# Packed attention with a mixture of experts on one core: the maxima's joining, the exponentials and the gates' chain moved among the work items

## The chip, the cores and the metric

The kernel runs on one core of a Trainium2 chip. The metric is the device time of one execution in microseconds (us). TensorE (PE), VectorE (DVE), ScalarE (ACT), GpSimd (POOL) and SyncE (SP, which issues most of the loads and stores) each work through their own list of instructions in order and wait for each other by semaphores. PEld in the views is TensorE's loading of weights, which runs beside its matmuls.

## The reference

```python
def sm_attn(qq, kk, vv):
    s = scale * np.matmul(qq, kk.transpose(0, 1, 3, 2))
    s = s - np.max(s, axis=-1, keepdims=True)
    a = np.exp(s)
    a = a / (np.sum(a, axis=-1, keepdims=True) + 1e-09)
    return np.matmul(a, vv)
p_packed = sm_attn(p, k, v)          # p: 32 rows a head; k, v: 576 rows
out = sm_attn(q, p_packed, p_packed) # 8 batches, 8 heads, 576 rows, 64 columns
...
logits = xn @ en.T / tau             # x: out as 4608 rows of 512
expert_idx = np.argmax(logits, axis=1)
...
h = np.maximum(x[mask] @ w1[e], 0.0)            # 512 -> 1024
out[mask] = gate_w[mask, None] * (h @ w2[e])    # 1024 -> 512
```

Everything is float32. xn and en are the normalised rows and expert embeddings; gate_w is the largest of the softmax over the 8 experts.

## The kernel before, in words

The eight batches are worked one after the other, and two of them overlap: while the FFN of batch b runs (the generator `ffn`), the attention of batch b+1 (`att_main`) is issued in small pieces between its pieces. `ffn` yields 56 times, once per **item**: 16 hidden items (8 blocks of 128 hidden units for each half of the 576 columns, 6 matmuls each, L979; the second half's items also leave 64 columns for later), 8 items for the last 64 rows (L1014), and 4 x 8 items for the second matrix (L1032). A hidden item is a group of matmuls into one of three PSUM banks (`pf`), a yield, then a ReLU on ScalarE (L983) and a subtraction on VectorE (L984), which leave the value as a rounded part and a rest.

The loop at the end of the kernel sets the order. After item n it takes a step of the next batch's attention, and from item `GATE` on a step of this batch's gates (`gates_main`):

```python
step_att(b + 1)
...
if gate is None and hasattr(bat[b], "lg") and n >= GATE:
    gate = gates_main(b)
if gate is not None:
    next(gate, None)
```

Each instruction goes to its engine's list in the order in which it is issued here; an engine never passes an instruction that waits. The loop's rounds for b = 1 to 6 carry a "quarter" attention (`att1`, its `pack`), for batches 2 to 7:

- `quarter_scores`: packed rows against turned keys (L326), in two two-bank PSUM tiles `pt`, one for each group g of four heads.
- `quarter_max`: the negated row maxima of a group (L338). The scores of a row lie in four partition quarters, so `whole_max` joins the quarters with six small VectorE instructions (L346 to L352) into `qnm`.
- `quarter_exp`: eight exponentials on ScalarE, four a group (L358). `quarter_flip`: GpSimd adds up parts of them (L374) and VectorE turns them (L375).
- `quarter_values`: matmuls with v (L385) and with the sums (L394); then the division, the pair rows (L477) and their turning (L487).
- In between, `next(queries)` turns a block of q into a `kt` tile on VectorE (L287), four in all. The fourth stands in the steps of `guess`, which adds up the logits (L611), finds the largest with MAX and MAX_INDEX (L617, L618), and writes `sel` (L622). The expert's number then starts the loads of its weights on GpSimd's queue (L869, L877).
- `query_scores` (L266) needs all four `kt` tiles. The softmax over the packed rows (L657 to L697), the route products (L747) with their reduction (L762), and the first FFN matrix folded with the packed rows (L912) follow.

`gates` computes the rows' gates for the FFN of the present batch: a reciprocal root in eleven small VectorE instructions (L92, L98, then three times L103, L105, L108; a yield after each third), a scaling and an exponential, a sum and its reciprocal. The first store of the batch (L1378, item 26) needs them. It takes seven steps.

Of the kernel before, what the change touches and what calls it, by code (L numbers as in the profile page):

```python
# [27 lines left out]
def kernel(  # L28
# [220 lines left out]
    def idle(n):  # L249
        for _ in range(n):  # L250
            yield
# [63 lines left out]
    def quarter_banks(x):  # L315
        for g in range(NG):
            x.s1[g] = pb.tile([P, 1024], F32, name="pt", tag="pb")
            nc.vector.memset(area(x, g)[64:P, :, :, :32], LOW)

    def quarter_scores(x):  # L320
        for r in range(NPR):
            for a in range(HB):
                at = RUNS[a] * 32 + (32 if a >= 2 else 0)
                n = QW - (32 if a >= 2 else 0)
                for u in range(2):
                    nc.tensor.matmul(  # L326
                        area(x, r // 2)[32 * a : 32 * a + 32, u, r % 2, QW - n :],
                        half_rows(x.pw, u)[:, r],
                        half_rows(x.kT[r], u)[:, at : at + n],
                        start=True,  # L330
                        stop=True,
                        tile_position=(64 * u, 32 * a),
                    )

    def quarter_max(x, g):
        if g == 0:
            x.qm = sm.tile([P, 2 * HB], F32, name="qm", tag="qm", bufs=1)
        nc.vector.tensor_reduce(  # L338
            x.qm[:, HB * g : HB * g + HB].rearrange("p (f s) -> p f s", f=2), area(x, g),
            axis=AX.X, op=ALU.max, negate=True,  # L340
        )

    def whole_max(x):

        low = sm.tile([64, 2 * HB], F32, name="qlow", tag="qlow", bufs=1)
        nc.vector.tensor_copy(low, x.qm[64:P])  # L346
        nc.vector.tensor_tensor(out=low, in0=x.qm[:64], in1=low, op=ALU.min)
        x.nm = sm.tile([P, 2 * HB], F32, name="qnm", tag="qnm", bufs=1)
        nc.vector.tensor_copy(x.nm[:32], low[32:64])
        nc.vector.tensor_tensor(out=x.nm[:32], in0=x.nm[:32], in1=low[:32], op=ALU.min)  # L350
        nc.vector.tensor_copy(x.nm[32:64], x.nm[:32])
        nc.vector.tensor_copy(x.nm[64:P], x.nm[:64])  # L352
# [133 lines left out]
    def pair_turn(x, g, pt):  # L486
        nc.tensor.transpose(  # L487
            pt[:, g * P : (g + 1) * P], pairs_of(x, g), ident
        )

    def pack_tiles(x):
        x.T = x.Tq = sm.tile([P, NG * P], F32, name="T", tag="T", bufs=1)
        x.ppx = sb.tile([P, NG, XW], F32, name="ppx", tag="ppx", bufs=2)
# [20 lines left out]
    def att1(x, nat, queries=None):  # L514

        def pack(queries):
            pack_tiles(x)
            if not x.s1:
                quarter_banks(x)
            quarter_scores(x)  # L520
            yield
            for g in range(NG):
                quarter_max(x, g)
                yield
            yield
            whole_max(x)
            yield from idle(2)
            for g in range(NG):
                for n in range(HB):
                    quarter_exp(x, g, n)  # L530
                    if n % 2:
                        yield
                quarter_flip(x, g)
            yield from idle(2)
            pt = pb.tile([P, 1024], F32, name="pt", tag="pb")
            sums = pt[:, NG * D : NG * D + NG * QW // 4].rearrange("p (g k) -> p g k", g=NG)
            for g in range(NG):
                quarter_values(x, g, nat(2 * NPR + g), pt[:, g * D : g * D + D], sums[:, g])
            next(queries)
            yield  # L540
            quarter_sums(x, sums)
            for g in range(NG):
                pair_rows(x, g, pt[:, g * D : g * D + D])
            yield
            pu = pc.tile([P, 512], F32, name="pu", tag="pu")
            for g in range(NG):
                pair_turn(x, g, pu)
            next(queries)
            yield
            nc.vector.tensor_copy(x.T, pu[:, 0 : NG * P])  # L550
            yield from idle(2)
            pt = pc.tile([P, 512], F32, name="pu", tag="pu")
            row_logits(x, pt)
            yield
            logits_out(x, pt)
            next(queries)
            yield

        def pack_slowly():
            pack_tiles(x)  # L560
            for g in range(NG):
                pt = pb.tile([P, 1024], F32, name="pt", tag="pb")
                p1_turn(x, g, pt)
                yield
                p1_evac(x, g, pt)
                key_sum(x, g)
                yield
            pt = pb.tile([P, 1024], F32, name="pt", tag="pb")
            for g in range(NG):
                pack_values(x, g, nat(2 * NPR + g), pt[:, g * D : g * D + D])  # L570
            yield
            for g in range(NG):
                pair_rows(x, g, pt[:, g * D : g * D + D])
            yield
            pu = pc.tile([P, 512], F32, name="pu", tag="pu")
            yield
            for g in range(NG):
                pair_turn(x, g, pu)
            yield
            nc.vector.tensor_copy(x.T, pu[:, 0 : NG * P])  # L580
            yield
            pt = pc.tile([P, 512], F32, name="pu", tag="pu")
            row_logits(x, pt)
            logits_out(x, pt)
            yield

        if x.halves:
            for g in range(NG):
                key_max(x, g)
                yield  # L590
                key_exp(x, g)
                yield
            yield from pack_slowly()
        else:
            asked = queries or all_queries(x, nat)
            yield from pack(asked)
            if queries is None:
                drain(asked)
# [797 lines left out]
        return store  # L1396

    WARM = (4, 4)
    GATE = 18


    ORDS = (
# [24 lines left out]
    with tc.manual_schedule():  # L1427
        begun = begin()
        soft = att_main(0)
        routing = route_first()  # L1430
        asked = all_queries(bat[1], nat_main(1))
        att = [(b, att_main(b)) for b in range(1, B)]

        done = [0] * (B + 1)

        def step_att(last):
            while att and att[0][0] <= last:
                try:
                    next(att[0][1])
                    done[att[0][0]] += 1  # L1440
                    return
                except StopIteration:
                    att.pop(0)

        gate = None

        def run(steps):
            nonlocal gate
            for c in steps:
                if c == "q":  # L1450
                    next(begun, None)
                elif c == "s":
                    next(soft, None)
                elif c == "G":
                    split_g(bat[0])
                elif c == "a":
                    step_att(1)
                elif c == "d":
                    next(asked, None)
                elif c == "w":  # L1460
                    split_w2(bat[0])
                elif c == "r":
                    assert bat[0].begun and bat[0].soft
                    next(routing, None)
                elif hasattr(bat[0], "lg"):
                    gate = gate or gates_main(0)
                    next(gate, None)

        run(PLAN[0])
        for b in range(B):  # L1470
            after = bat[b + 1] if b + 1 < B else None
            work = ffn(
                bat[b], store_main(b), late=b == 0, after=after, end=b == B - 1,
                between=lambda: run("q"),
            )
            for n, _ in enumerate(work):
                if b == 0:
                    run(PLAN[n + 1] if n + 1 < len(PLAN) else "srag")
                    continue
                if n == 0:  # L1480
                    gate = None
                step_att(b + 1)
                if n >= DBL and done[b + 1] < n - LAG:
                    step_att(b + 1)
                if gate is None and hasattr(bat[b], "lg") and n >= GATE:
                    gate = gates_main(b)
                if gate is not None:
                    next(gate, None)


    nc.vector.tensor_scalar(
# [7 lines left out]
    with tc.If(n_rest > 0):  # L1499
        with tc.For_i(0, B, 1) as b:  # L1500
            nb = nc.values_load(rest_i[0:1, ds(b, 1)], min_val=0, max_val=S)
            with tc.If(nb > 0):
                x = Batch()
# [85 lines left out]
```

## Time and profile before

| | |
|---|---|
| median of 3 runs | 438.03 us (437.65 to 439.3) |
| the profiled execution | 436.4 us, span 434.8 us |
| busy, share of the span | PE 96%, PEld 76%, DVE 73%, ACT 46%, POOL 35% |
| chain that ended last | PE 75%, DVE 13%, DMA 3% |
| granted TensorE clock, mean | 0.995 |
| HBM traffic | 200 GB/s over the span |

The profiled execution's time holds its span and 1.6 us around it. Times of trace rows are us from the span's start.

### The profile page before, as it was taken

The page shows a single profiled execution, that of the slowest core. Times are in us where ns is not written, and L with a number is a line of the kernel's source. Part 1 is how long each engine was busy: PE and PEld are TensorE (multiplying, and loading weights), DVE is VectorE, ACT ScalarE, POOL GpSimd, SP SyncE. Part 2 cuts the span into 40 slices and gives each one's busy share as a digit, 9 for nine tenths or more (in the row PEclk, how much of TensorE's full clock was granted, in tenths as well). Part 3 has the DMA queues.
Part 4 walks back from the last instruction along what each step waited for, and adds up shares of the span by engine and source line. Part 5 has one row for each costly group of instructions (what it writes and reads, how often), then busy time and mean ns, then how long its engine had stood idle before and what let it go on. Part 6 is the DMA issues. An engine that isn't in the chain of part 4 may idle for free.

```text
span 434.8 us, 11089 instructions
## 1 busy us (share of the span) xinstructions
PE 418.2 (96%) x4094; PEld 330.1 (76%) x4095; DVE 319.1 (73%) x930; ACT 200.2 (46%) x472; POOL 154.0 (35%) x177
## 2 busy tenths in 40 slices
PE   7999999999999999999999999999999999999993
PEld 4758677796868868698777968788686987779783
DVE  3577696688967889779977889678897799466500
ACT  4557615662265614663146622656146631476110
POOL 2345813436313551325314362135513253141200
PEclk9999999999999999999999999999999999999997
DMA  8999896957989489973999579794898707410011
GB/s 224 323 256 269 213 293 232 246 155 201 348 235 214 112 252 332 215 191 96 263 335 222 138 195 348 233 215 118 250 335 211 195 4 289 160 36 14 23 49 46
DMA packets 42223, 87.92 MB, mean 202 GB/s; under 512 B 11306, under 2 KB 20522, under 8 KB 42162
## 3 DMA queue, kind: packets, MB, share of 16 engines
q1 hardware_dynamic: 34896, 61.44, 53.0%
q0 software_dynamic: 6720, 25.17, 16.8%
q10 hardware_dynamic: 546, 0.54, 0.6%
q8 instruction: 34, 0.56, 0.6%
q14 instruction: 27, 0.22, 0.2%
HBM read 77.68 MB, written 9.44 MB: 200 GB/s over the span
## 4 chain that ended last, share of the span: by engine, by line
PE 75%; DVE 13%; DMA 3%; SPq 3%; ACT 2%; issue 2%; DVEq 0%; ACTq 0%
PE pf L1032 41%; PE pf L979 14%; PE pt L747 5%; PE pt L912 3%; DVE hT L984 3%; DVE kt L287 3%; PE pf L1014 2%; PE pt L266 2%; DMA pn<-in_p 2%; PE pt L326 2%; SPq L194 1%; DVE p1T L375 1%; PE pf L1177 1%; ACT hT L983 1%; SPq L233 1%
## 5 line engine op out<-in xcount | busy, mean ns | idle before, releaser
L1032 PE MATMUL pf<-w2s,hT 128*128 128x512 f32 (+1 forms) x792 | 184.0, 388 | 0.0
L1032 PEld LDWEIGHTS pf<-w2s,hT 128*128 128x128 f32 x792 | 143.1, 188 | 39.6 <-issue 10.7
L888 POOL TENSOR_TENSOR w2s<-w2r,w2s 128x512 fp32r<-128x512 f32 x64 | 80.8, 1284 | 107.8 <-ACT w2s L887 73.6
L979 PE MATMUL pf<-AT,G 128*128 128x288 f32 x720 | 104.8, 299 | 1.8 <-DVE hT L984 1.7
L979 PEld LDWEIGHTS pf<-AT,G 128*128 128x128 f32 x720 | 97.8, 188 | 6.4 <-DVE hT L984 3.9
L983 ACT ACTIVATE hT<-pf 128x224 fp32r<-128x224 f32 (+1 forms) x128 | 49.4, 386 | 48.3 <-PE pf L979 47.2
L984 DVE SCALAR_TENSOR_TENSOR hT<-pf,hT 128x224 fp32r<-128x224 f32 (+1 forms) x128 | 52.2, 413 | 21.0 <-ACT hT L983 20.4
L1378 ACT ACTIVATE o<-pf,gate 128x512 f32<-128x512 f32 (+1 forms) x41 | 26.0, 633 | 33.8 <-PE pf L1032 21.9
L287 DVE STREAM_TRANSPOSE kt<-nat 128x576 f32<-128x576 f32 x52 | 38.2, 761 | 0.6 <-DMA nat<-in_q 0.6
L887 ACT CAST w2s<-w2r 128x512 fp32r<-128x512 f32 x64 | 38.6, 616 | 0.0
L759 ACT ACTIVATE scr<-pt 128x512 f32<-128x512 f32 (+2 forms) x47 | 25.0, 531 | 23.1 <-PE pt L747 22.2
L1014 PE MATMUL pf<-w2r,h 128*64 128x256 f32 x256 | 33.3, 388 | 0.0
L374 POOL TENSOR_TENSOR qs<-p 128x320 f32<-128x320 f32 x12 | 10.6, 881 | 49.6 <-ACT p L358 49.6
L762 DVE TENSOR_REDUCE lg<-pt 128x8 f32<-128x32 f32 (+2 forms) x47 | 8.6, 182 | 26.1 <-ACT scr L759 25.9
L671 ACT ACTIVATE st<-st 128x576 f32<-128x576 f32 (+1 forms) x17 | 11.1, 657 | 34.4 <-DVE st L668 32.6
L697 POOL TENSOR_TENSOR AT<-at,AT 128x576 fp32r<-128x576 f32 x7 | 10.0, 1424 | 44.7 <-ACT AT L692 44.7
L850 ACT ACTIVATE lg<-lg 128x40 f32<-128x40 f32 x8 | 1.9, 237 | 50.0 <-DVE lg L846 50.0
L747 PEld LDWEIGHTS pt<-ppx,at 64*128 64x128 f32 (+1 forms) x320 | 19.4, 175 | 7.1 <-issue 3.6
L747 PE MATMUL pt<-ppx,at 64*128 64x136 f32 (+1 forms) x320 | 24.3, 290 | 0.0
L1014 PEld LDWEIGHTS pf<-w2r,h 128*64 128x64 f32 x256 | 19.4, 137 | 4.9 <-issue 1.8
L692 ACT CAST AT<-at 128x576 fp32r<-128x576 f32 x15 | 10.1, 673 | 22.7 <-DVE at L686 22.7
L877 POOL DMA_DIRECT2D w2r<-in_moe_w x24 | 16.9, 711 | 0.0
(205 smaller groups left out, 492.6 us busy)
## 6 DMA issues: line engine op xcount, KB each, us to landing
nat<-in_q SPq DMA_DIRECT2D x112, 140.0 KB, 3.3
nat<-in_k SPq DMA_DIRECT2D x96, 140.0 KB, 3.6
w1t<-in_moe_w POOLq DMA_DIRECT2D x12, 1024.0 KB, 9.7
w2r<-in_moe_w POOLq DMA_DIRECT2D x24, 512.0 KB, 12.7
out<-o SPq DMA_DIRECT2D x124, 64.0 KB, 3.0
vn<-in_v SPq DMA_DIRECT2D x48, 160.0 KB, 4.8
w2r<-in_moe_w SPq DMA_DIRECT2D x8, 512.0 KB, 9.7
nat<-in_k SPq DMA_DIRECT2D x4, 576.0 KB, 7.6
```

Of the source, the lines that this page charges most:

```text
L287: nc.vector.transpose(kt.rearrange("p (c i) -> p c i", i=32), t)
L747: nc.tensor.matmul(to[: rows(c), half], x.at[at, g, c * P : c * P + rows(c)], x.ppx[at, g], start=True, stop=True, tile_position=(64 * hal ...
L759: nc.scalar.activation(scr[:r, :, : pt.shape[2]], pt[:r, :, :, : 2 * D], AF.Square, accum_out=sss[:r])
L877: queue.dma_start(t, w2e[:, 2 * i : 2 * i + 2, :])
L887: nc.scalar.copy(t[:, 0], raw)
L888: nc.gpsimd.tensor_tensor(out=t[:, 1], in0=raw, in1=t[:, 0].bitcast(F32), op=ALU.subtract)
L979: nc.tensor.matmul(pf[:, :HS], w, r, start=(n == 0), stop=(n == len(ops) - 1))
L983: nc.scalar.activation(hT[:, 0, f, cs], pf[:, :n], AF.Relu)
L984: nc.vector.scalar_tensor_tensor(out=hT[:, 1, f, cs], in0=pf[:, :n], scalar=0.0, in1=hT[:, 0, f, cs].bitcast(F32), op0=ALU.max, op1=ALU.su ...
L1014: nc.tensor.matmul(pf[64 * hf : 64 * hf + 64, :256], h4[:, f], x.w2r[f // 2][:, f % 2, hf * 256 : hf * 256 + 256], start=(f == 0), stop=(f ...
L1032: nc.tensor.matmul(pf[:, :w], hT[:, a, f, c * P : (c + 1) * P], x.w2s[f][:, m, at : at + w], start=(f == 0 and i == 0), stop=(f == NF - 1 ...
L1378: nc.scalar.activation(o[:, :w], pf[:, :w], AF.Copy, scale=x.gate[:, c : c + 1])
```

## The change

The two `quarter_max` steps stand together in one item. `whole_max` becomes a generator with a yield in its middle: three joining instructions in one item, three in the next. The exponentials of a group are issued as two, one, one over three items and not as two and two over two. One idle item before `quarter_values` goes, and one before the exponentials moves ahead, so `quarter_values` stays in its item (12). The gates' chain begins at item 21 and not 18, and takes two steps an item from item 22 on, so that it ends in item 24 as before.

```diff
         x.nm = sm.tile([P, 2 * HB], F32, name="qnm", tag="qnm", bufs=1)
         nc.vector.tensor_copy(x.nm[:32], low[32:64])
+        yield
         nc.vector.tensor_tensor(out=x.nm[:32], in0=x.nm[:32], in1=low[:32], op=ALU.min)
...
             for g in range(NG):
                 quarter_max(x, g)
-                yield
-            yield
-            whole_max(x)
+            yield
+            yield from whole_max(x)
             yield from idle(2)
             for g in range(NG):
                 for n in range(HB):
                     quarter_exp(x, g, n)
-                    if n % 2:
+                    if n:
                         yield
                 quarter_flip(x, g)
-            yield from idle(2)
+            yield
...
-    GATE = 18
+    GATE = 21
...
-                if gate is not None:
-                    next(gate, None)
+                for _ in range(1 + (n > GATE)):
+                    if gate is not None:
+                        next(gate, None)
```

How this moves instructions, at three places of one round of the loop. (Lines from 350 on are one higher in the changed kernel, so L351 there is L350 before.) First VectorE at the hidden items 0 to 7: `hT` is an item's subtraction, `qm` the maxima, `qlow` and `qnm` their joining. Before:

```order
L984 SCALAR_TENSOR_TENSOR hT<-pf,hT 128x288
L338 TENSOR_REDUCE qm<-pt 128x4
L984 SCALAR_TENSOR_TENSOR hT<-pf,hT 128x288
L338 TENSOR_REDUCE qm<-pt 128x4
L984 SCALAR_TENSOR_TENSOR hT<-pf,hT 128x288 x2
L346 COPY qlow<-qm 64x8
L347 TENSOR_TENSOR qlow<-qm,qlow 64x8
L349 COPY qnm<-qlow 32x8
L350 TENSOR_TENSOR qnm<-qnm,qlow 32x8
L351 COPY qnm<-qnm 32x8
L352 COPY qnm<-qnm 64x8
L984 SCALAR_TENSOR_TENSOR hT<-pf,hT 128x288 x4
```

With the change:

```order
L984 SCALAR_TENSOR_TENSOR hT<-pf,hT 128x288
L338 TENSOR_REDUCE qm<-pt 128x4 x2
L984 SCALAR_TENSOR_TENSOR hT<-pf,hT 128x288
L346 COPY qlow<-qm 64x8
L347 TENSOR_TENSOR qlow<-qm,qlow 64x8
L349 COPY qnm<-qlow 32x8
L984 SCALAR_TENSOR_TENSOR hT<-pf,hT 128x288
L351 TENSOR_TENSOR qnm<-qnm,qlow 32x8
L352 COPY qnm<-qnm 32x8
L353 COPY qnm<-qnm 64x8
L984 SCALAR_TENSOR_TENSOR hT<-pf,hT 128x288 x5
```

The second maximum moves ahead of item 1's subtraction, and the six joining instructions, which stood together ahead of item 4's, stand three ahead of item 2's and three ahead of item 3's.

Second, VectorE at items 18 to 22: `kt` are the third and the fourth turned block of q, `rq_` and `gy` the gates' chain, the rest the guess. Before:

```order
L287 STREAM_TRANSPOSE kt<-nat 128x576
L92 TENSOR_SCALAR rq_i<-ss 128x5
L98 TENSOR_SCALAR rq_h<-ss 128x5
L103 TENSOR_TENSOR rq_t<-rq_h,rq_i 128x5
L105 TENSOR_TENSOR rq_t<-rq_t,rq_i 128x5
L108 SCALAR_TENSOR_TENSOR gy<-rq_t,rq_i 128x5
L103 TENSOR_TENSOR rq_t<-rq_h,gy 128x5
L617 MAX m_1658<-pu 1x8
L618 MAX_INDEX idx<-m_1658,pu 1x8
L620 CAST gi<-idx 1x1
L622 TENSOR_SCALAR sel<-ecol,gi 1x8
L287 STREAM_TRANSPOSE kt<-nat 128x576
```

With the change:

```order
L287 STREAM_TRANSPOSE kt<-nat 128x576
L617 MAX m_1648<-pu 1x8
L618 MAX_INDEX idx<-m_1648,pu 1x8
L620 CAST gi<-idx 1x1
L622 TENSOR_SCALAR sel<-ecol,gi 1x8
L287 STREAM_TRANSPOSE kt<-nat 128x576
L92 TENSOR_SCALAR rq_i<-ss 128x5
L98 TENSOR_SCALAR rq_h<-ss 128x5
L103 TENSOR_TENSOR rq_t<-rq_h,rq_i 128x5
L105 TENSOR_TENSOR rq_t<-rq_t,rq_i 128x5
L108 SCALAR_TENSOR_TENSOR gy<-rq_t,rq_i 128x5
L103 TENSOR_TENSOR rq_t<-rq_h,gy 128x5
```

The six gate instructions that stood between the third block of q and the guess now stand behind the fourth block.

Third, ScalarE at the hidden items from 0 to 11: `hT` are the ReLUs, `p` the exponentials of the two groups. Before:

```order
L983 ACTIVATE hT<-pf 128x288 x6
L358 ACTIVATE p_1411<-pt,qnm 128x160 x2
L983 ACTIVATE hT<-pf 128x288
L358 ACTIVATE p_1411<-pt,qnm 128x160 x2
L983 ACTIVATE hT<-pf 128x288
L358 ACTIVATE p_1439<-pt,qnm 128x160 x2
L983 ACTIVATE hT<-pf 128x224
L358 ACTIVATE p_1439<-pt,qnm 128x160 x2
L983 ACTIVATE hT<-pf 128x224 x4
```

With the change:

```order
L983 ACTIVATE hT<-pf 128x288 x5
L359 ACTIVATE p_1402<-pt,qnm 128x160 x2
L983 ACTIVATE hT<-pf 128x288
L359 ACTIVATE p_1402<-pt,qnm 128x160
L983 ACTIVATE hT<-pf 128x288
L359 ACTIVATE p_1402<-pt,qnm 128x160
L983 ACTIVATE hT<-pf 128x288
L359 ACTIVATE p_1439<-pt,qnm 128x160 x2
L983 ACTIVATE hT<-pf 128x224
L359 ACTIVATE p_1439<-pt,qnm 128x160
L983 ACTIVATE hT<-pf 128x224
L359 ACTIVATE p_1439<-pt,qnm 128x160
```

The first pair stands one ReLU earlier, and the eight exponentials are spread over six items instead of four.

## Rows read from the trace of the kernel before

**Rows 1.** Busy time of the engines, sum over six loop rounds of 50.8 us, 83.5 to 388.3

```profile
sum 304.80, PE 299.34 PEld 239.15 DVE 249.04 ACT 141.68 POOL 113.05; mean PE 49.89 PEld 39.86 DVE 41.51 ACT 23.61 POOL 18.84
```

**Rows 2.** Who waited for whom, whole span: us in total, times, longest

```profile
PEld pt L266 <- DVE rq_t L105: 7.0, 6, 1.2
...
PE pt L266 <- DVE rq_t L105: 3.8, 6, 0.6
...
PE pf L979 <- DVE hT L984: 1.7, 6, 0.3
```

**Rows 3.** Timeline of VectorE, one round: start, us, line, instruction, [idle before <- releaser]

```profile
203.41 0.78 DVE L287 STREAM_TRANSPOSE kt<-nat 128x576 f32<-128x576 f32 x1
204.11 0.76 DVE L92 TENSOR_SCALAR rq_i<-ss 128x5 int32<-128x5 int32 x1
...
205.65 0.15 DVE L617 MAX8 m<-pu 1x8 f32<-1x8 f32 x1
...
206.46 0.78 DVE L287 STREAM_TRANSPOSE kt<-nat 128x576 f32<-128x576 f32 x1
```

**Rows 4.** Timeline of TensorE's weight loads, the same round

```profile
205.97 0.17 PEld L266 LDWEIGHTS pt<-kt,T 64*32 64x32 f32 x12 [0.38 <-issue]
207.29 0.63 PEld L266 LDWEIGHTS pt<-kt,T 64*32 64x32 f32 x20 [1.15 <-DVE rq_t L105]
208.38 0.77 PEld L1032 LDWEIGHTS pf<-w2s,hT 128*128 128x128 f32 x4 [0.47 <-issue]
```

**Rows 5.** Timeline of TensorE, the last matmul of the guess

```profile
204.07 0.20 PE L611 MATMUL pu<-ppx,itaus 128*64 128x8 f32 x1
```

**Rows 6.** Timeline of TensorE's weight loads, the query scores of batch 1

```profile
53.76 0.67 PEld L266 LDWEIGHTS pt<-kt,T 64*32 64x32 f32 x32 [0.38 <-issue]
54.89 0.20 PEld L1014 LDWEIGHTS pf<-w2r,h 128*64 128x64 f32 x4 [0.46 <-issue]
```

**Rows 7.** Timeline of VectorE, the hidden items 1 to 5 of the round

```profile
186.90 0.82 DVE L338 TENSOR_REDUCE qm<-pt 128x4 f32<-128x640 f32 x1
188.76 0.46 DVE L984 SCALAR_TENSOR_TENSOR hT<-pf,hT 128x288 fp32r<-128x288 f32 x1 [1.03 <-ACT hT L983]
...
189.87 0.93 DVE L984 SCALAR_TENSOR_TENSOR hT<-pf,hT 128x288 fp32r<-128x288 f32 x2
190.83 0.17 DVE L346 COPY qlow<-qm 64x8 f32<-64x8 f32 x1
...
192.00 0.82 DVE L984 SCALAR_TENSOR_TENSOR hT<-pf,hT 128x288 fp32r<-128x288 f32 x2
```

**Rows 8.** Timeline of TensorE, the hidden items 1 to 6 and 7 to 12

```profile
187.22 5.01 PE L979 MATMUL pf<-AT,G 128*128 128x288 f32 x36
192.51 5.14 PE L979 MATMUL pf<-AT,G 128*128 128x288 f32 x36 [0.28 <-DVE hT L984]
```

**Rows 9.** Timeline of ScalarE, the first two exponentials of the round

```profile
192.00 0.68 ACT L358 ACTIVATE p<-pt,qnm 128x160 f32<-128x160 f32 x2
```

**Rows 10.** Timeline of VectorE, the second turning of the probabilities

```profile
196.12 0.83 DVE L375 STREAM_TRANSPOSE p1T<-p 128x640 f32<-128x640 f32 x1
```

**Rows 11.** Timelines of VectorE and TensorE at the route products

```profile
223.68 0.19 DVE L762 TENSOR_REDUCE lg<-pt 128x8 f32<-128x32 f32 x1 [0.45 <-ACT scr L759]
...
225.64 1.81 PE L747 MATMUL pt<-ppx,at 64*128 64x136 f32 x24
```

**Rows 12.** One line's instructions, whole span: times, ns min/median/max, first and last start

```profile
L92 DVE TENSOR_SCALAR rq_i<-ss x8: 151/763/782, 56.1 to 402.4; 128x5 int32<-128x5 int32 x8
...
L843 DVE TENSOR_SCALAR gy<-gy x8: 171/332/350, 59.5 to 406.8; 128x5 f32<-128x5 f32 x8
```

**Rows 13.** Timeline of GpSimd, the same round

```profile
202.32 2.52 POOL L888 TENSOR_TENSOR w2s<-w2r,w2s 128x512 fp32r<-128x512 f32 x2
207.14 1.52 POOL L869 DMA_DIRECT2D w1t<-in_moe_w  x2 [2.30 <-DVE sel L622]
```

**Rows 14.** Timeline of SyncE's queue, the load of the fourth block of q

```profile
191.04 1.84 SPq L194 DMA_DIRECT2D nat<-in_q x4
```

## The prediction

> **What bounds the kernel now.** I read the table of busy time by stretch first. Six stretches of 50.8 us each, one for every FFN pass that runs beside a "quarter" attention (batches 1 to 6), hold 304.80 of the 434.8 us, and in them TensorE is busy 49.89 us of each 50.8 [rows 1]. So TensorE sets the time, and no change that leaves its instructions alone can gain more there than its idle time and what its matmuls lose around that. The order of TensorE, GpSimd and SyncE is the same in both programs; only VectorE's and ScalarE's orders move.
>
> The table of waits says where TensorE stands idle: six times before the query scores (L266), 3.8 us in all for its matmuls and 7.0 us for its weight loads, and six times before a hidden matmul (L979), 1.7 us in all [rows 2]. Once a loop each, and nothing else of weight. Both are waits for VectorE, so the question is what VectorE does just before. The page names L105 as the releaser of the first, which is only the next instruction on VectorE; the tile that L266 reads is kt.
>
> **The gates' chain.** In the timeline of VectorE (the round of b = 3; the other five agree to 0.1 us) the third query transpose runs at 203.41, then six instructions of the gates' chain, of which the first starts at 204.11, then the guess (MAX at 205.65), and only then the fourth transpose, 206.46 to 207.24 [rows 3]. TensorE loads its first query weights at 205.97, gets through 12 of 32, and stands still for 1.15 us until 207.29 [rows 4]. With the gates begun three items later, the guess and the transpose stand ahead of the chain. MAX then waits for the later of two things: the end of the third transpose (204.11) and the last guess matmul, 204.07 + 0.20 = 204.27 [rows 5], say 204.32. That is 1.33 us earlier, so the fourth transpose ends at 207.24 - 1.33 = 205.91. TensorE arrives at 205.97 and needs that tile only after 12 loads (0.17 us): a margin of 0.06 + 0.17 = 0.23 us. The stall goes.
>
> What is it worth? From the first of these loads to the first load of the next work is 208.38 - 205.97 = 2.41 us [rows 4]. The same 32 loads of the same function, unhindered in batch 1, take 54.89 - 53.76 = 1.13 us [rows 6]. The difference is 1.28 us. From below stand the idle time of the matmuls alone, 3.8 / 6 = 0.63 us, and of the loads, 7.0 / 6 = 1.17 us [rows 2]. I take 1.28, since it is measured from end to end over the same work, and keep 0.63 as the poor end. Doubling the gate steps after item 21 adds no instruction: the chain ends in item 24 in both orders, and VectorE's work in between is the same.
>
> **The maxima.** TensorE has three banks for its hidden items, so item n+3 needs VectorE's subtraction (L984) of item n. Before, the six small joining instructions (L346 to L352) run together, 190.83 to 192.00, that is 0.195 us each; item 4's subtraction starts only behind them, and TensorE waits 0.28 us for it at 192.51 [rows 7, 8]. Now both maxima (0.82 us each) stand in item 1: 186.90 + 1.64 = 188.54, inside the time in which VectorE waits 1.03 us for item 1's ReLU anyway, until 188.76 [rows 7]. So the second maximum costs nothing there. Its subtraction ends at 189.22; three joining instructions later, at 189.80, item 2's follows (189.87 before). Three more, and item 3's runs from 190.85 to 191.31. TensorE does items 1 to 6 in 5.01 us from 187.22, 0.835 each, so it needs item 3's at 191.40 (margin 0.09) and item 4's, now about 191.8, at 192.23 (margin 0.4) [rows 8]. The 0.28 us goes; if the thin margin fails, a tenth comes back. I count 0.28 and keep 0 as the other end.
>
> **The exponentials.** ScalarE does the same eight, in pairs of 0.68 us [rows 9], but over six items and not four, and the first pair one item earlier: it needs the joined maxima, there at about 190.85, and item 4's ReLU stands ahead of it on ScalarE anyway. Per item its extra load falls from 0.68 to (0.68 + 0.34 + 0.34) / 3 = 0.45 us. The ReLUs come no later than now, so nothing is added. The second turn of the probabilities (L375, 0.83 us) moves one item nearer to the matmuls that read it. It was done at 196.95 [rows 10]; one item later, less the 0.28, is 196.95 + 0.835 - 0.28 = 197.5. TensorE comes to those matmuls at 192.51 + 5.14 - 0.28 = 197.37 [rows 8], and begins with the other group, half of the work. So I cost this at nothing, with some 0.2 us to spare.
>
> **The sum.** Six loops x (1.28 + 0.28) = 9.4 us. The profiled execution took 436.4 us, so it would take 427.0. The median of the three timed runs, 438.03, stands 1.6 us above it, and by that the median after is **428.6 us**.
>
> **What is late next.** With 1.28 us less on TensorE behind the guess, VectorE's softmax comes closer to it. TensorE's second group of route products starts at 225.64 and needs the banks that the reduction at 223.68 + 0.19 = 223.87 frees [rows 11]: 1.77 us of room, of which 1.77 - 1.28 = 0.49 is left, and 0.28 if VectorE idles 0.21 us (204.11 to 204.32) before MAX. There is a second effect. The first gate instruction (L92) takes 0.763 us in the median and 0.151 at best [rows 12], and in this loop it ends at 204.87, with GpSimd's tensor_tensor (202.32 + 2.52 = 204.84) [rows 3, 13]. It looks held, not busy. Behind the fourth transpose, at 205.9, it meets no such instruction, and VectorE gets some 0.6 us back: 0.28 + 0.6 = 0.9 us of room. The Trainium skill states this in GPSIMD Engine Reference, Key points: GpSimd shares its SBUF interfaces with VectorE, and there is contention with VectorE instructions in a two-port mode or with two SBUF inputs. By that rule the room is 0.9 and not 0.28 us, and the sum stays; without it I would give the first rival 0.25 and not 0.15.
>
> **Rivals.**
> - *VectorE takes over in part (0.15).* The margins of 0.09, 0.23 and 0.28 us are not all kept, and a new wait of about 0.5 us a loop stands before the route products or the query scores. 9.4 - 6 x 0.5 = 6.4 us: 431.6 us. For it: VectorE works almost without a gap from 203.41 to 223.87. Against it: the 0.6 us of L92.
> - *The change does not do what it says (0.06).* The fourth transpose may wait not for its place on VectorE but for its block of q. Then only the maxima's 6 x 0.28 = 1.7 us goes: 436.3 us, no change that can be told. Against it: that load is issued from 191.04, 15 us before [rows 14].
> - *Slower (0.04).* GpSimd's weight-load issues (two in load_w1, four in load_w2) begin at 207.14, when the guess is known [rows 13], now at 205.8, so that nearly all of the gates' chain, of which most instructions read two operands in SBUF, runs beside them. If each of the six holds VectorE as the tensor_tensor held L92, that is 6 x 0.6 = 3.6 us; less the room of 0.28, TensorE waits 3.3 us a loop before the route products and gains 1.56: 6 x 1.8 = 10.6 us more, 448.6 us. It decides from 0.28 + 1.56 = 1.8 us a loop on. The rule of the Trainium skill named above (GPSIMD Engine Reference, Key points) could be read so. Against it: L843 runs beside these issues now, and its median is 0.332 us against 0.171 at best [rows 12], a loss of 0.16 us and not 0.6; six of that are 1.0 us, about the room.
>
> **How the numbers follow.** The forecast has 0.72, the rivals 0.15, 0.06 and 0.04; 0.03 is left for what I do not see. The forecast's own range: 1.17 to 1.28 for the query scores and 0.2 to 0.3 for the maxima give 8.2 to 9.5 us, and with runs that differ by about 0.8 us, 427.5 to 430.5. To take in the first rival and a slightly larger gain I go from 427.0 to 432.2; the poor end of 0.63 us a loop (438.03 - 6 x 0.91 = 432.6) lies just beyond. A change under 0.5% (2.2 us) is about what a measurement of this kernel can't tell from none. Faster by more: 0.72 + 0.15 + 0.02 = 0.89. Within: 0.07. Slower: 0.04.
>
> **What would show it.** Right: the six stretches are 49.2 us long; in the waits TensorE's two entries are gone or below 0.1 us each time; the 32 query-score loads follow each other in about 0.7 us; on VectorE MAX stands directly behind the third transpose and L92 takes under 0.4 us; VectorE no longer idles 1.03 us after the first maximum. Wrong: TensorE waits before L747 for the reduction at L762 or before L385 for the transpose at L375, L266 still waits for kt, or the gates' instructions take 0.3 us and more each beside GpSimd's loads.

## The result, and the profile after

| | before | with the change |
|---|---|---|
| median of 4 runs each, same chip | 437.84 us (436.83 to 439.3) | 425.94 us (425.51 to 426.19) |
| ratio, 95% interval | | 0.9725 (0.9696 to 0.9754) |
| profiled execution | 436.4 us, span 434.8 | 425.83 us, span 424.1 |
| six loop rounds, mean | 50.80 us | 49.10 us |
| chain that ended last | PE 75%, DVE 13% | PE 93%, DVE 2% |

The kernel is 2.75% faster, as forecast in sign and mechanism, but the time lies 1.1 us under the low end of the range (427.0). Of the profiled span's 10.7 us, 304.80 - 294.60 = 10.2 us lie in the six rounds. Busy time of the engines in the first and the fifth round and the sum over six (columns: stretch, its length, busy us and count of each engine, then granted TensorE clock, DMA share and GB/s), which answers to [rows 1]:

```profile
83.20:132.23 49.03, 49.03 (x508) 39.77 (x507) 41.20 (x115) 23.69 (x56) 18.86 (x22) 1.00 0.83 230
...
279.47:328.69 49.22, 49.22 (x508) 40.02 (x508) 41.33 (x116) 23.69 (x56) 18.82 (x22) 1.00 0.83 230
...
sum 294.60, PE 294.60 PEld 238.65 DVE 244.53 ACT 142.14 POOL 113.06; mean PE 49.10 PEld 39.77 DVE 40.75 ACT 23.69 POOL 18.84
```

TensorE's busy time now equals the length of the rounds: no idle time of its matmuls is left in them. The waits of TensorE say the same. Before, L266 and L979 led that list with six waits each [rows 2]; what leads it now lies in the opening, before the rounds:

```profile
PE pf L1165 <- DVE mask L72: 1.2, 1, 1.2
```

VectorE behind the third block of q, in the round that [rows 3] show (it now begins at 181.28, not 185.1):

```profile
199.12 0.78 DVE L287 STREAM_TRANSPOSE kt<-nat 128x576 f32<-128x576 f32 x1
200.02 0.16 DVE L617 MAX8 m<-pu 1x8 f32<-1x8 f32 x1
...
200.84 0.78 DVE L287 STREAM_TRANSPOSE kt<-nat 128x576 f32<-128x576 f32 x1
201.54 0.13 DVE L92 TENSOR_SCALAR rq_i<-ss 128x5 int32<-128x5 int32 x1
```

From the third transpose's start to the fourth's it now takes 200.84 - 199.12 = 1.72 us, before 206.46 - 203.41 = 3.05: 1.33 us earlier, as worked out. TensorE's weight loads for the query scores run through, against the stop of 1.15 us in [rows 4]:

```profile
201.69 0.67 PEld L266 LDWEIGHTS pt<-kt,T 64*32 64x32 f32 x32 [0.38 <-issue]
202.82 1.23 PEld L1032 LDWEIGHTS pf<-w2s,hT 128*128 128x128 f32 x6 [0.46 <-issue]
```

They take 202.82 - 201.69 = 1.13 us up to the next work, the value of the unhindered batch [rows 6]. VectorE at the maxima, against [rows 7]:

```profile
183.06 1.55 DVE L338 TENSOR_REDUCE qm<-pt 128x4 f32<-128x640 f32 x2
184.92 0.46 DVE L984 SCALAR_TENSOR_TENSOR hT<-pf,hT 128x288 fp32r<-128x288 f32 x1 [0.30 <-ACT hT L983]
...
185.99 0.46 DVE L984 SCALAR_TENSOR_TENSOR hT<-pf,hT 128x288 fp32r<-128x288 f32 x1
...
186.94 0.82 DVE L984 SCALAR_TENSOR_TENSOR hT<-pf,hT 128x288 fp32r<-128x288 f32 x2
```

The second maximum fills the wait for item 1's ReLU, of which 0.30 of 1.03 us is left. The subtractions of items 2 and 3 start at 185.99 and 186.94, and nothing is late: all 72 matmuls of items 1 to 12 are now one stretch, where [rows 8] show two with a gap.

```profile
183.38 10.00 PE L979 MATMUL pf<-AT,G 128*128 128x288 f32 x72
```

The two gate instructions of [rows 12], over the whole span:

```profile
L92 DVE TENSOR_SCALAR rq_i<-ss x8: 128/129/273, 55.8 to 391.9; 128x5 int32<-128x5 int32 x8
L843 DVE TENSOR_SCALAR gy<-gy x8: 170/172/175, 59.2 to 396.2; 128x5 f32<-128x5 f32 x8
```

L92's median fell from 763 to 129 ns without a change to the instruction.

### The profile page after: what moved, and what is told of

It is laid out like the page before. It is cut to its first block, busy times and chain, and to the rows that moved or that the text cites. A ratio compares the mean times of both kernels' runs of the same rounds, so it can differ in the third digit from the quotient of the medians.

```text
span 424.1 us, 11083 instructions
## 1 busy us (share of the span) xinstructions
PE 412.6 (97%) x4094; PEld 329.0 (78%) x4095; DVE 314.6 (74%) x930; ACT 200.7 (47%) x472; POOL 154.1 (36%) x177
## 4 chain that ended last, share of the span: by engine, by line
PE 93%; DVE 2%; DMA 2%; ACT 1%; issue 0%; SPq 0%; ACTq 0%
PE pf L1032 42%; PE pf L979 24%; PE pf L1014 7%; PE pt L747 5%; PE pt L912 3%; PE pt L266 2%; PE pt L386 2%; PE pt L326 2%; DMA nat<-in_k 1%; PE pf L1177 1%; PE pt L451 1%; PE pt L1209 0%; PE pu L488 0%; PE pf L947 0%; PE pu L499 0%; PE pf L464 0%
## 5 line engine op out<-in xcount | busy, mean ns | idle before, releaser
L1032 PEld LDWEIGHTS pf<-w2s,hT 128*128 128x128 f32 x792 | 143.1, 188 | 39.7 <-issue 10.7
L979 PE MATMUL pf<-AT,G 128*128 128x288 f32 x720 | 103.8, 299 | 0.1
L979 PEld LDWEIGHTS pf<-AT,G 128*128 128x128 f32 x720 | 97.7, 188 | 3.9 <-issue 1.2
L747 PEld LDWEIGHTS pt<-ppx,at 64*128 64x128 f32 (+1 forms) x320 | 19.4, 175 | 7.3 <-issue 3.6
L762 DVE TENSOR_REDUCE lg<-pt 128x8 f32<-128x32 f32 (+2 forms) x47 | 8.6, 183 | 21.6 <-ACT scr L759 21.5
L747 PE MATMUL pt<-ppx,at 64*128 64x136 f32 (+1 forms) x320 | 24.4, 290 | 0.1
L692 ACT CAST AT<-at 128x576 fp32r<-128x576 f32 x15 | 10.2, 677 | 22.6 <-DVE at L686 22.6
L359 ACT ACTIVATE p<-pt,qnm 128x160 f32<-128x160 f32 x48 | 17.8, 399 | 0.0
```

The costliest lines, as they stand in the source:

```text
L359: nc.scalar.activation(x.p1[g][:, n * QW : n * QW + QW], area(x, g)[:, n // 2, n % 2], AF.Exp, bias=x.nm[:, at : at + 1],)
L747: nc.tensor.matmul(to[: rows(c), half], x.at[at, g, c * P : c * P + rows(c)], x.ppx[at, g], start=True, stop=True, tile_position=(64 * hal ...
L979: nc.tensor.matmul(pf[:, :HS], w, r, start=(n == 0), stop=(n == len(ops) - 1))
L1032: nc.tensor.matmul(pf[:, :w], hT[:, a, f, c * P : (c + 1) * P], x.w2s[f][:, m, at : at + w], start=(f == 0 and i == 0), stop=(f == NF - 1 ...
```

## The experiments

The runs compare the rounds first, since their mean repeats between two profiles of the kernel before (50.80 and 50.81 us) and the whole time does not. A round is read from the chain of waits: it shows the start of the first route products (L747) in each round, and the sixth start less the first, divided by five, is the mean round. The kernel before, and the changed one:

```profile
118.67 1.13 PE pt L747 x16
...
372.65 1.13 PE pt L747 x16
```

```profile
116.56 1.13 PE pt L747 x16
...
362.11 1.13 PE pt L747 x16
```

That is 253.98 / 5 = 50.80 and 245.55 / 5 = 49.11 us. The other runs' mean rounds are got in the same way.

| run | what it is | mean round, us | less than before | median, us | ratio to before (interval) |
|---|---|---|---|---|---|
| e1_control | the kernel before | 50.81 | 0 | 436.51 | 0.9998 (0.9972 to 1.0024) |
| e2_gates | gates' chain alone | 49.54 | 1.26 | 429.24 | 0.9805 (0.9778 to 0.9833) |
| e3_attention | attention's part alone | 50.38 | 0.42 | 434.98 | 0.9934 (0.9911 to 0.9957) |
| e4_maxima | the same, exponentials in pairs | 50.45 | 0.35 | 434.14 | 0.9939 (0.9918 to 0.996) |
| e5_gate19 | changed kernel, chain from item 19 | 49.77 | 1.03 | 430.6 | 0.9888 (0.9844 to 0.9932) |
| e6_pad3 | changed kernel, 3 memsets a round | 49.12 | 1.68 | 425.12 | 0.975 (0.9725 to 0.9775) |
| e7_pad9 | changed kernel, 9 memsets a round | 49.83 | 0.97 | 430.9 | 0.9895 (0.9856 to 0.9934) |
| e8_joined | changed kernel, joining in one piece | 49.54 | 1.26 | 428.39 | 0.9827 (0.9801 to 0.9854) |

The first four ran on one chip beside 23 runs of the kernel before (median 437.19), the last four on another beside 9 (435.75).

**e1_control: the kernel before against itself.** No edit.

> The kernel before, unchanged, as a control. The prediction added 1.6 us to a profiled execution to get a median. Theory: the kernel before varies from run to run by 2 us and more, and its first profile (436.4 us) was an execution at the low end, so the offset belongs to that one draw. Then the ratio is 1.00 within its interval, the profiled execution here lies anywhere from 436 to 439.5 us, and if it is a long one its six loop rounds, not the part before them, are longer than 50.8 us. Rival: timed runs stand a fixed 1.6 us above a profiled one; then the profile is 436.4 again, and the changed kernel's should have been 424.3 and not 425.83 us.

Twelve runs spread from 435.38 to 440.12 us; the profiled one took 435.61. That is 0.4 us under the range given for it. The rounds are those of the first profile (50.81 against 50.80). So the fixed offset is refuted: this profile stands 0.9 us under its median, the first 1.4 us under the median of its four runs, the changed kernel's 0.1 us under, and that of the run with only the attention's part 1.1 us above (436.11 against 434.98). The theory's guess was that a long execution has longer rounds. The control's profile was a short one; in all the profiles, what differs most beside the edits is the opening. The chain shows where the query scores of batch 1 begin, at the end of it, here in the control and in the run with only the attention's part:

```profile
53.28 1.13 PE pt L266 x32
```

```profile
56.50 1.13 PE pt L266 x32
```

Over the profiles of the eight runs and the two main ones it begins between 53.28 and 56.50 us. What is left of each profiled time beyond this start and six mean rounds lies between 77.1 and 77.8 us, so the opening varies by 3.2 us and the rest by 0.7. No execution of the kernel before above 436.4 us was profiled; that its longest ones, up to 440.12 us, are long by their openings is not shown. What the opening waits for differs (in the attention's run loads of w1 and of k stand in the chain); which load sets it was not tried.

**e2_gates: the gates' chain alone.** The kernel before with

```diff
-    GATE = 18
+    GATE = 21
...
-                if gate is not None:
-                    next(gate, None)
+                for _ in range(1 + (n > GATE)):
+                    if gate is not None:
+                        next(gate, None)
```

> Only the gates' chain moved (item 21, two steps an item), the maxima, joining and exponentials as before. Theory: the wait for the fourth query transpose goes alone, six times 1.28 us = 7.7 us: 430.1 us, loop rounds of 49.5 us, L266's loads without a stop, the wait of L979 for L984 still 0.3 us in each round, L92 at 0.13 us. Rival: the two parts need each other (VectorE is late for the one as long as it is late for the other); then the gain is under 6 us and a wait before L266 stays.

The round is 1.26 us shorter, against 1.28 worked out, and 6 x 1.26 = 7.6 of the forecast 7.7 us. TensorE waits no more before L266; the hidden items' wait stays as it was:

```profile
PE pf L979 <- DVE hT L984: 1.7, 6, 0.3
```

The rival, that the parts need each other, falls. The median is 429.24 where 430.1 was expected, 0.9 us less, which is within what the opening varies.

**e3_attention: the attention's part alone.** The changed kernel with the loop and GATE = 18 of the kernel before.

> Only the attention's part (both maxima together, joining in two parts, exponentials two, one, one), the gates' chain from item 18 as before. Theory: the stretch from the first quarter scores to the values falls from 10.31 to 9.94 us, six times 0.37 = 2.2 us: 435.6 us, and the wait before L266 stays at 0.6 us of the matmuls and 1.15 us of the loads in each round. Rival: what is gained there is lost at L266, since the gates' instructions now meet the fourth transpose as before and VectorE sets both; then no change, 437.8 us, and the wait before L266 is 0.9 us and more.

The round is 0.42 us shorter, a little more than the 0.37 expected, and L266 waits as before:

```profile
PE pt L266 <- DVE rq_t L105: 3.8, 6, 0.7
```

So nothing is lost again at L266. The two parts add up: 1.26 + 0.42 = 1.68 us a round, and the whole change has 1.69.

**e4_maxima: the exponentials left in pairs.** Against the run before:

```diff
-            yield from idle(2)
+            yield from idle(3)
...
-                    if n:
+                    if n % 2:
                         yield
                 quarter_flip(x, g)
-            yield
+            yield from idle(2)
```

> Like the run with only the attention's part, but the exponentials in pairs over four items from item 6, as before. Theory A: the joining alone held TensorE, in the listed wait of 0.28 us and some 0.1 us of shorter ones; then the stretch is 9.94 us here too, and the time that of the run with the spread exponentials. Theory B: 0.28 us is the joining's and 0.1 us that of the paired exponentials, which make ReLUs late; then the stretch is 10.03 us and the time some 0.5 us above that run's.

The stretch between the quarter scores and the values, read from the chain, first with pairs:

```profile
85.49 1.13 PE pt L326 x48
96.64 0.69 PE pt L386 x40
```

then in the last round of the run with the exponentials spread:

```profile
339.11 1.13 PE pt L326 x48
...
350.18 0.70 PE pt L386 x40
```

96.64 - 86.62 = 10.02 us and 350.18 - 340.24 = 9.94 us. Theory B's stretch came: the pairs cost 0.08 us a round here, 0.07 by the mean round, and the maxima and their joining give 0.35. Its time did not come: the median is 0.8 us below the other run's and not 0.5 above (434.14 against 434.98). The medians can't tell 0.4 us; the openings outweigh it.

**e5_gate19: the first three instructions of the gates' chain ahead of the guess again.** The changed kernel with

```diff
-    GATE = 21
+    GATE = 19
```

> The changed kernel with the gates' chain from item 19 on and not 21: its first three instructions (L92, L98, L103) stand between the third query transpose and the guess again. It tells apart what L92's 0.76 us was. Theory: GpSimd's tensor_tensor holds L92; here L92 would start about 0.76 us before that instruction ends, takes 0.7 to 0.8 us again and ends with it, the fourth transpose ends some 0.7 us after TensorE needs it, the rounds last 49.8 us and not 49.1, and the time is 430.3 us. Rival: L92 is long only by its place in the first rounds, and the three take 0.5 us in all; then the transpose ends within 0.1 us of the need, the rounds last 49.1 to 49.2 us, and the time is 426.2 us.

The theory's numbers came: rounds of 49.77 us and 430.6 us. VectorE, then GpSimd and TensorE's loads, in one round:

```profile
201.84 0.76 DVE L92 TENSOR_SCALAR rq_i<-ss 128x5 int32<-128x5 int32 x1
...
203.60 0.78 DVE L287 STREAM_TRANSPOSE kt<-nat 128x576 f32<-128x576 f32 x1
```

```profile
198.82 3.76 POOL L888 TENSOR_TENSOR w2s<-w2r,w2s 128x512 fp32r<-128x512 f32 x3 [1.16 <-PE pu L488]
```

```profile
203.71 0.17 PEld L266 LDWEIGHTS pt<-kt,T 64*32 64x32 f32 x12 [0.39 <-issue]
204.43 0.63 PEld L266 LDWEIGHTS pt<-kt,T 64*32 64x32 f32 x20 [0.56 <-DVE rq_t L105]
```

L92 takes 0.76 us again and ends at 202.60, with GpSimd's last tensor_tensor (198.82 + 3.76 = 202.58). Behind the fourth transpose the same instruction takes 0.13 us. GpSimd was not taken away in a run, so the cause is argued; but in the kernel before and here the end of the one follows the end of the other by some 0.03 us in each of the six rounds.

**e6_pad3 and e7_pad9: how much room VectorE has.** At the end of the gates, in each of the six rounds, three or nine instructions of no use are added:

```diff
+        if 0 < b < B - 1:
+            pad = sm.tile([P, NPR, 32], F32, name="pad", tag="pbd", bufs=1)
+            for _ in range(9):
+                nc.vector.memset(pad, 0.0)
```

> The changed kernel with three more VectorE instructions (memsets of a dead tile, 0.5 to 0.6 us in all) behind the gates' chain in each of the six rounds, ahead of the softmax. They ask how much room VectorE has before TensorE's second group of route products; the trace of the changed kernel shows 1.1 us there. Theory: no change, 425.9 us, rounds of 49.1 us. Rival: VectorE already sets the time behind the guess; then each round grows by the 0.55 us, and the time is 429.2 us.

No change, rounds of 49.12 us: the three memsets take 0.68 us in a round, and even so VectorE does not set the time.

> The same with nine memsets, 1.6 to 1.8 us in each round. Theory: the room of 1.1 us is used up and the rest, 0.5 to 0.7 us, stands as a wait of TensorE before L747 for L762 in each round: 429 to 430.2 us, rounds of 49.6 to 49.8 us. Rival A: there is more room than the trace shows (the banks aren't what L747 waits for); then 425.9 us. Rival B: VectorE sets the time already; then 1.7 us a round, 436.1 us.

The time is 430.9, the rounds 49.83 us, both just above what the theory gave (430.2 and 49.8). The nine took 2.23 us and not 1.8 (each starts 0.26 us after the one ahead, though one takes 0.165), so more was added than meant. And the wait stands elsewhere than expected. VectorE, then TensorE:

```profile
209.18 2.23 DVE L1375 MEMSET pad<- 128x128 f32 x9
...
217.72 0.78 DVE L686 STREAM_TRANSPOSE at<-st 128x576 f32<-128x576 f32 x1
```

```profile
218.64 1.20 PE L747 MATMUL pt<-ppx,at 64*128 64x136 f32 x16 [0.75 <-DVE at L686]
```

TensorE waits before the *first* group of route products, for the first half of the softmax's turned result, 0.7 us a round. The room was 2.23 - 0.72 (49.83 - 49.11) = 1.5 us. The changed kernel's trace has that number in this pair of rows:

```profile
212.31 0.78 DVE L686 STREAM_TRANSPOSE at<-st 128x576 f32<-128x576 f32 x1
```

```profile
214.63 1.20 PE L747 MATMUL pt<-ppx,at 64*128 64x136 f32 x16
```

214.63 - 213.09 = 1.54 us.

**e8_joined: the joining of the maxima in one piece.** The changed kernel with

```diff
         nc.vector.tensor_copy(x.nm[:32], low[32:64])
-        yield
         nc.vector.tensor_tensor(out=x.nm[:32], in0=x.nm[:32], in1=low[:32], op=ALU.min)
...
-            yield from whole_max(x)
-            yield from idle(2)
+            whole_max(x)
+            yield from idle(3)
```

> The changed kernel with the joining of the maxima in one piece again, all six instructions in item 2, one idle item more, the exponentials in their new place. It tells apart the two edits on the maxima. Theory: the cut in two is what keeps TensorE going; six instructions (1.17 us) in one place make item 2's subtraction end about 0.3 us too late for item 5, so the rounds last 49.4 us and the time is 427.7 us. Rival: bringing both maxima into item 1 is enough, since the joining then starts earlier; then the rounds last 49.1 us and the time is 425.9 us.

Rounds of 49.54 us: to the hundredth the gates' chain alone. (Lines from 350 on are those of the kernel before, less one from 523 on.) VectorE, then TensorE:

```profile
187.72 0.17 DVE L346 COPY qlow<-qm 64x8 f32<-64x8 f32 x1
...
188.88 1.19 DVE L983 SCALAR_TENSOR_TENSOR hT<-pf,hT 128x288 fp32r<-128x288 f32 x3
```

```profile
189.40 6.71 PE L978 MATMUL pf<-AT,G 128*128 128x288 f32 x48 [0.28 <-DVE hT L983]
```

Six instructions in one place put item 2's subtraction at 188.88, and TensorE waits 0.28 us for it two items earlier than it did before. With the joining in one piece, bringing the maxima together and spreading the exponentials gain nothing; the cut in two is worth 49.54 - 49.11 = 0.43 us a round, the whole of the attention's part. Whether the cut would do it with the maxima left apart was not tried.

## Why the prediction was right or wrong

**What bounds the kernel: right.** TensorE's order is unchanged, its two waits are gone from every round, and its idle time in the rounds fell from (304.80 - 299.34) / 6 = 0.91 us each to none. That idle time is 5.5 of the 10.2 us gained there. The other 4.7 us are busy time, 299.34 against 294.60 for the same instructions: in the profile's count, part of what a stop costs is not idle but busy time.

**The query scores, 1.28 us a round: right**, 1.26 alone. The end-to-end reading of the same 32 loads was the right one to take; the idle time of the matmuls (0.63) and of the loads (1.17) were too small. The margin of 0.23 us was as thin as worked out: in the fifth round of the changed kernel VectorE loses 0.19 us inside the guess, in a pause for which the profile names no other engine, and the query scores take 301.14 - 299.87 = 1.27 and not 1.13 us; that round is the one of 49.22.

```profile
298.67 0.16 DVE L618 FIND_INDEX8 idx<-m,pu 1x8 uint32<-1x8 f32 x1 [0.19 <-issue]
```

```profile
299.87 0.81 PEld L266 LDWEIGHTS pt<-kt,T 64*32 64x32 f32 x32 [0.39 <-issue]
301.14 1.00 PEld L1032 LDWEIGHTS pf<-w2s,hT 128*128 128x128 f32 x5 [0.47 <-issue]
```

**The maxima, 0.28 us a round: right in kind, too small.** It was read from the listed wait alone, while the whole attention's part is worth 0.42. Measured over the same stretch from end to end, as for the query scores, it would have been known: from item 1's matmuls at 187.22 to the end of item 12's at 192.51 + 5.14 = 197.65 is 10.43 us before [rows 8], and twice the 5.01 us of the first six items is 10.02, 0.41 less. (The 72 matmuls take 10.00 us in the changed kernel.) All of it is the one stop. The last matmul ahead of it, in the kernel before:

```profile
191.94 0.29 PE L979 MATMUL pf<-AT,G 128*128 128x288 f32 x1
```

The next begins at 192.51, 0.57 us later. In one stretch a matmul begins 10.00 / 72 = 0.14 us after the one ahead, so the stop costs 0.43 us; the list counts it from the end of the last matmul, 191.94 + 0.29 = 192.23, and has 0.28.

**The exponentials, nothing: right against the old order only.** The new order adds no wait, as forecast. But I compared it only with the old order as it stood, where the stop for the joining stands ahead. Once the joining is cut, exponentials left in pairs cost 0.07 us a round (e4); while it is in one piece, spreading them gains nothing (e8). So 0.07 of the 0.42 us needs both edits.

**The sum, and the step that failed.** Two terms of it failed: the 0.28 us of the maxima, and the 1.6 us from the profile to the median. 6 x (1.28 + 0.28) = 9.4 us stands against 10.2 in the rounds, 0.8 us too little: the term of 0.28, which measured 0.42. Another 0.4 us went outside the rounds; the opening of the changed kernel's profile is 0.34 us shorter (the query scores of batch 1 begin at 53.49 and not 53.83), no more than it varies between executions of one kernel (53.83 and 53.28). So the profiled execution took 425.83 us and not 427.0. The larger part of the miss is the next sentence of the prediction: "The median of the three timed runs, 438.03, stands 1.6 us above it, and by that the median after is 428.6 us". It carried over an offset that changes from draw to draw. The changed kernel's median stands 0.1 us above its profiled execution, the control's 0.9, and that of e3 1.1 us below. Runs of the kernel before go from 435.15 to 440.12 us in all. The four runs of the changed kernel lie within 0.7 us, and those of e6 too, while those of the kernel before beside them spread over 2.5 and 2.6; whether that is chance or the change narrows it stays open. Of the 2.7 us between forecast and median, 1.5 are this offset and 1.2 the sum. The range was closed at 427.0 from the same median, with 0.8 us for the runs, where the three runs known then spread over 1.65. On another chip, the changed kernel with three idle memsets stands at 0.975 and not 0.9725 of the kernel before: 435.75 - 425.12 = 10.6 us, which is nearer to the 10.2 of the rounds than the first comparison's 11.9.

**What is late next: half right.** VectorE had room, and L92 gave it 0.63 us back (763 to 129 ns), as forecast from its end at GpSimd's end. e5 puts L92 beside GpSimd's instruction again, and it is long again: 0.76 us beside GpSimd's tensor_tensor, 0.13 us without it. The Trainium skill states in GPSIMD Engine Reference, Key points, that GpSimd shares its SBUF interfaces with VectorE, with contention for VectorE instructions in a two-port mode or with two SBUF inputs. The trace agrees in kind: L92 is long only where it meets GpSimd's instruction, and ends with it. But L92 reads one tensor (ss), and in which mode it ran no run shows.

But the place was wrong. I named the second group of route products and the reduction at L762. In e7, with VectorE late, that group starts before the reduction has ended (224.18 + 0.19 = 224.37), and it takes the same 1.81 us as in [rows 11]: it does not wait for it.

```profile
224.07 1.81 PE L747 MATMUL pt<-ppx,at 64*128 64x136 f32 x24
```

```profile
224.18 0.19 DVE L762 TENSOR_REDUCE lg<-pt 128x8 f32<-128x32 f32 x1 [0.45 <-ACT scr L759]
```

The pair that binds first is the first group and the transpose at L686, with 1.5 us of room.

**The rivals.** VectorE taking over in part: no; 0.68 us more on it cost nothing (e6), though 2.23 us did (e7). The fourth transpose held by its load: no, it moved with its place. Slower by GpSimd's weight loads: no. In the changed kernel the loads' issues and the gates' chain do run side by side, and the chain's instructions take 0.13 to 0.20 us each; L843, which I had charged with 0.16 us beside them, takes 0.17 us in all. But this has to do with when it starts. In five of the six rounds before it ends with a load issue (208.32 + 0.34 = 208.66, and the two at L869 end at 207.14 + 1.52 = 208.66 [rows 13]), and in e5 in all six, where it takes 0.35 to 0.45 us. In the changed kernel's round it starts at 203.78, 0.06 us after an issue has begun. So an issue may hold an instruction of this form; the rival's six times 0.6 us did not come.

## What to carry to other kernels

A stall's price is read from end to end over the same work at a place where it is not hindered: the listed idle time was less than the stop cost in both places here (0.63 of 1.26 us, 0.28 of 0.43). On a strict queue, small instructions that nobody waits for yet belong behind the one for which the bounding engine waits, and a cluster of them belongs in pieces between the releases of its buffers. Before an offset between profile and timed runs is added to a forecast, ask which part of the execution varies; in the profiles here it was the opening, and the sum belonged to the rounds alone.

## What the runs showed of the hardware that was not expected

- An instruction of 128 x 5 elements took 0.76 us in place of 0.13 for where it stood, next to a GpSimd instruction with which it shares no data. L843 takes 0.332 us in the median before and 0.172 after, although GpSimd issues loads beside it in both; when it is long it ends with the end of a load issue. No run took the issues away.
- The query scores' 20 loads behind the stop take 208.38 - 207.29 = 1.09 us to the next work [rows 4], nearly as much as all 32 in one go (1.13): a stop of 1.15 us costs 1.26, though 12 loads were done ahead of it.
- The mean round repeats to 0.01 us between the two profiles of the kernel before (50.80 and 50.81), while whole runs of it differ by up to 4.7 us on one chip (435.38 to 440.12).
